# Guards behind operations that read the same data, decayed keys in a buffer of their own, score halves ahead of the next decay part

## Chip, cores and metric

The kernel runs on 1 core of one Trainium2 chip. The metric is the device time of one launch in microseconds (us); lower is better. Differences of about 1% are what a measurement of this kernel can tell from no change.

## What is computed

Three layers over 4 sequences of 768 tokens, 8 heads of 48: a gated linear attention, a dense SiLU layer and a layer of 8 experts of which each token takes one.

```python
for t in range(S):                       # attention, per batch and head
    state = alpha[t, :, None] * state + outer(k[t], v[t])
    y[t] = q[t] @ state
h = x @ w_in                             # x: y of all heads, 3072 x 384
x2 = (h * sigmoid(h)) @ w_out            # d_ff 2048
e = argmax(norm(x2) @ norm(expert_emb).T / tau)
out = gate * (relu(x2 @ w1[e]) @ w2[e])  # 8 experts, 1024 wide
```

## The kernel before

The engines are PE (matrix), DVE (vector), ACT (scalar), POOL (GpSimd) and SP, which issues DMAs. Numbers are kept as pairs of fp16 parts (high and low), so a product is three matmuls.

**Stages.** The dense layer goes over 8 blocks of 384 tokens (`block(j)`), each with 16 steps f: `mm1` makes 128 columns of h (9 matmuls), ACT forms the SiLU and its high part, DVE the low part (line 1084), `mm2` multiplies by w_out (9 matmuls). Attention goes over 24 chunks n of 128 tokens of one sequence; three chunks make one block of x. Chunks 0 to 2 run alone at the start; the others are put between the dense steps: `att_steps` is a generator, and `pump` advances it at up to two points of each f, so the attention of later blocks runs while PE multiplies for the present one. Weights of w_in and w_out are converted in block 0 (`Conv`), those of the experts from block 2 on (`weight1`, `weight2`: a DMA into a staging tile, then `split_after`: ACT makes the high part, DVE the low part). After block 7 follow the expert tiles.

**One chunk** (from chunk 6 on, `n >= NF`, parts in fp16). `att_C`: scores of K and Q into two PSUM banks, ACT copies them to S, POOL sets the upper triangle to zero. `att_S`: ACT and DVE split S into `ss`. `att_A` of the *next* chunk: transpose of alpha (PE), the running product P (DVE scan), its inverse R (DVE), two ACT reductions of P and R into `junk` for a range check (`att_G`), the end factors `pe` (POOL). `att_Bk`, `att_Bq`: transposes of k and q, K = k·R and Q = q·P on DVE. `att_KT`: POOL multiplies K in place by the end factor, ACT and POOL split it into `kd`, and a DMA transposes `kd` into KT. `att_D`: output yp = qs·st + ss·vs. `att_U`: the state update up = KT·vs. Seven steps (yields) per chunk: C; A of n+1 with S and KT of n; Bk; D first half; D second half; move, V and Bq; U.

**What sets the order.** Each engine runs its instructions in one fixed row. The rows are made when the program is built, by a scheduler that goes by the order of the program and its own estimates of when data will be there; `behind(ins, before)` forces an order within an engine. A reduction into a `guard` table (is the data in the range the fp16 parts can hold?) is an ordinary instruction in such a row. For every third chunk `att_V` puts three reductions of the freshly loaded q, k, v tiles (`guard_nat`, line 801); `weight1` puts one for each of the 8 experts' first staging tiles (`guard_w`, line 682). PSUM tiles of the attention come from one pool of three banks in turn (`bank`): a new tile waits until the one three before it has been read.

## Time and profile before

| | |
|---|---|
| time before, median of 3 runs | 791.33 us (789.27 to 795.85) |
| the profiled execution | 792.25 us, of which the span of the profile is 790.6 us |
| PE matmul busy | 748.7 us (95%), 5554 records |
| DVE / ACT / POOL busy | 496.2 / 413.0 / 223.5 us |
| mean granted TensorE clock | 0.991 of full speed |

The span runs from the first to the last instruction. A busy PE is not PE at its peak: ends of matmuls are modelled. "Idle before, releaser" names what ended a wait. Lines are those of the kernel before.

### The profile page before, as it was taken

The page shows a single profiled execution, that of the slowest core. Times are in us where ns is not written, and L with a number is a line of the kernel's source. Part 1 is how long each engine was busy: PE and PEld are TensorE (multiplying, and loading weights), DVE is VectorE, ACT ScalarE, POOL GpSimd, SP SyncE. Part 2 cuts the span into 40 slices and gives each one's busy share as a digit, 9 for nine tenths or more (in the row PEclk, how much of TensorE's full clock was granted, in tenths as well). Part 3 has the DMA queues.
Part 4 walks back from the last instruction along what each step waited for, and adds up shares of the span by engine and source line. Part 5 has one row for each costly group of instructions (what it writes and reads, how often), then busy time and mean ns, then how long its engine had stood idle before and what let it go on. Part 6 is the DMA issues. An engine that isn't in the chain of part 4 may idle for free. (4 is left out here: it accounts for less than half of the span.)

```text
span 790.6 us, 16507 instructions
## 1 busy us (share of the span) xinstructions
PE 748.7 (95%) x5554; PEld 469.7 (59%) x5554; DVE 496.2 (63%) x1446; ACT 413.0 (52%) x931; POOL 223.5 (28%) x322
## 2 busy tenths in 40 slices
PE   7888999999989899999999999999899999999995
PEld 5756777676656566656756655555345555555553
DVE  6599966787677977987877597485761212121211
ACT  3455655666655756766766695577532222222221
POOL 3301113554443553445243112041142111111101
PEclk9999999999999999999999999999999999999998
DMA  9699222444356545645432356157667665676562
GB/s 192 143 287 300 50 55 57 94 89 83 88 117 108 108 109 115 136 101 112 102 96 72 92 172 202 41 161 204 163 162 171 127 112 120 112 119 114 118 104 45
DMA packets 241100, 97.94 MB, mean 124 GB/s; under 512 B 222041, under 2 KB 230398, under 8 KB 240880
## 3 DMA queue, kind: packets, MB, share of 16 engines
q1 hardware_dynamic: 237424, 85.58, 50.2%
q0 software_dynamic: 3584, 11.18, 4.2%
q8 instruction: 51, 0.84, 0.4%
q14 instruction: 41, 0.34, 0.1%
HBM read 58.39 MB, written 12.16 MB: 89 GB/s over the span
## 5 line engine op out<-in xcount | busy, mean ns | idle before, releaser
L1098 PE MATMUL o<-wo_h,w2l 128*128 128x392 f16 x528 | 146.7, 331 | 2.1 <-DVE w2l L1084 1.8
L1426 DVE SCALAR_TENSOR_TENSOR work<-hp,work 128x512 f16<-128x512 f32 x56 | 38.7, 692 | 143.3 <-ACT work L1425 143.3
L1075 PE MATMUL hp<-w2l,wi_h 128*128 128x384 f16 x480 | 120.3, 326 | 0.0
L1098 PEld LDWEIGHTS <-w2l 128*128 128x128 f16 x792 | 75.9, 98 | 51.4 <-DVE w2l L1084 3.0
L1419 PE MATMUL hp<-w1h,xT 128*128 (+1 forms) x384 | 100.0, 379 | 4.6 <-DVE work L1426 3.1
L1075 PEld LDWEIGHTS <-wi_h 128*128 128x128 f16 x768 | 73.8, 98 | 48.4 <-issue 2.0
L1098 PE MATMUL o<-wo_l,w2l 128*128 128x392 f16 x264 | 87.5, 331 | 0.0
L1419 PEld LDWEIGHTS <-xT 128*128 128x128 f16 (+1 forms) x576 | 50.2, 101 | 61.7 <-issue 7.1
L1075 PE MATMUL hp<-w2l,wi_l 128*128 128x384 f16 x240 | 78.2, 326 | 0.0
L1458 POOL DMA_INDIRECT out_dram<-ob,mt x28 | 27.8, 993 | 168.4 <-ACT ob L1455 158.8
L1075 PE MATMUL hp<-w2h,wi_h 128*128 128x384 f16 x288 | 70.6, 326 | 2.4 <-DMA w2h<-ys 1.2
L1425 ACT ACTIVATE work<-hp 128x512 f16<-128x512 f32 x56 | 33.4, 597 | 73.1 <-PE hp L1419 62.9
L1084 DVE SCALAR_TENSOR_TENSOR w2l<-w2l 128x384 f16<-128x384 f32 x88 | 51.8, 591 | 24.5 <-ACT w2l L1083 24.2
L1098 PE MATMUL o<-wo_h,g 128*128 128x392 f16 x240 | 65.8, 329 | 0.3 <-DVE g L1084 0.2
L1419 PE MATMUL hp<-w1l,xT 128*128 (+1 forms) x192 | 63.7, 379 | 0.0
L1455 ACT ACTIVATE ob<-po,s 128x384 f32<-128x384 f32 x28 | 16.3, 581 | 86.1 <-PE po L1447 78.6
L1082 ACT ACTIVATE w2l<-hp 128x384 f32<-128x384 f32 x88 | 42.6, 484 | 31.8 <-PE hp L1075 28.4
L1075 PEld LDWEIGHTS <-wi_l 128*128 128x128 f16 x384 | 37.5, 98 | 24.6 <-DVE wi_l L585 1.9
L1098 PEld LDWEIGHTS <-g 128*128 128x128 f16 x360 | 34.6, 98 | 23.4 <-DVE g L1084 1.1
L1083 ACT ACTIVATE w2l<-w2l 128x384 f16<-128x384 f32 x88 | 45.6, 522 | 4.5 <-PE o L1098 3.0
L841 POOL TENSOR_SCALAR_AFFINE_SELECT S<-S 128x512 f32<-128x512 f32 x48 | 32.7, 705 | 52.8 <-ACT S L840 52.6
L1447 PEld LDWEIGHTS <-work 128*128 128x128 f16 (+1 forms) x384 | 33.5, 101 | 23.6 <-DMA work<-work 1.5
(309 smaller groups left out, 1578.1 us busy)
## 6 DMA issues: line engine op xcount, KB each, us to landing
work<-in_moe_w_dram SPq DMA_DIRECT2D x24, 512.0 KB
work<-in_moe_w_dram SPq DMA_DIRECT2D x30, 384.0 KB
w1h<-in_moe_w_in_dram SPq DMA_DIRECT2D x6, 768.0 KB
nat_a<-in_alpha_dram SPq DMA_DIRECT2D x23, 192.0 KB
nat_k<-in_k_dram SPq DMA_DIRECT2D x23, 192.0 KB
nat_q<-in_q_dram SPq DMA_DIRECT2D x23, 192.0 KB
nat_v<-in_v_dram SPq DMA_DIRECT2D x23, 192.0 KB
w1h<-in_moe_w_out_dram SPq DMA_DIRECT2D x5, 768.0 KB
```

The costliest lines, as they stand in the source:

```text
L841: nc.gpsimd.affine_select(out=s, in_=s, pattern=[[0, NPAIR], [1, 128]], compare_op=ALU.is_ge, fill=0.0, base=0, channel_multiplier=-1,)
L1075: ins = nc.tensor.matmul(out=hp, lhsT=wi[a][f // 2][:, c, (f % 2) * 128:(f % 2 + 1) * 128], rhs=x[:, c, :], start=(n == 0), stop=(n == 3 * ...
L1082: nc.scalar.activation(out=g, in_=hp, func=ACTF.Silu, scale=1.0 / (SX * SWI))
L1083: lead["a"] = nc.scalar.activation(out=gh, in_=g, func=ACTF.Copy, scale=SG)
L1084: lead["g"] = nc.vector.scalar_tensor_tensor(out=gl, in0=g, scalar=SG, in1=gh, op0=ALU.mult, op1=ALU.subtract)
L1098: nc.tensor.matmul(out=acc[t], lhsT=a[:, ts], rhs=wo[w][f // 2][:, f % 2, :], start=(f == 0 and n == 0), stop=(f == KF - 1 and n == 2),)
L1419: nc.tensor.matmul(out=hp[ts], lhsT=xT[:, a, ts], rhs=w1s[w][c][:, e if isinstance(e, int) else bass.ds(e, 1), fs], start=(n == 0), stop=( ...
L1425: lead["a"] = nc.scalar.activation(out=hs[:, 0], in_=hp, func=ACTF.Relu)
L1426: lead["g"] = nc.vector.scalar_tensor_tensor(out=hs[:, 1], in0=hp, scalar=0.0, in1=hs[:, 0], op0=ALU.max, op1=ALU.subtract)
L1447: nc.tensor.matmul(out=po[ts], lhsT=hT[c // 4][:, at + ts.start:at + ts.stop], rhs=w2s[w][c][:, e if isinstance(e, int) else bass.ds(e, 1) ...
L1455: nc.scalar.activation(out=ob, in_=po, func=ACTF.Copy, scale=d["fac"], accum_out=guard("finite", 0.0, ALU.not_equal))
L1458: lead["o"] = nc.gpsimd.indirect_dma_start(out=out[:, :], out_offset=bass.IndirectOffsetOnAxis(ap=d["row"], axis=0), in_=ob, in_offset=Non ...
```

## The change

No operation is added or removed: on every engine the same instructions stand in another order, and the DMAs are the same.

1. *Guards.* The reductions of q, k, v are now ordered `behind` the operation that reads the same tile (`seen`), and those of the experts' weights behind the low part of their split. The two reductions of P and R (`att_G`) are issued after Bq instead of inside A, and behind the latest SiLU high part.
2. *Decayed keys.* `att_KT` for fp16 chunks becomes `att_Kd` (the product, into a buffer `Kd` of its own, right after Bk) and `att_kd` (the split and the DMA transpose, in the step of D's first half), both for chunk n+1 during chunk n; K goes from two buffers to one.
3. *Score halves.* `att_S(n)` stands ahead of `att_A(n + 1)`, and `att_Bq` is a step of its own ahead of D, with the split of Q and of the state (`att_Bs`) left where Bq was. A chunk has eight steps.

```diff
--- before.py
+++ after.py
@@ -622,7 +622,7 @@
                         )
                 hi, lo = wo["h"][self.i][:, :, DM:NA], wo["l"][self.i][:, :, DM:NA]
                 nc.scalar.activation(out=hi, in_=self.pl, func=ACTF.Copy)
-                nc.vector.tensor_sub(out=lo, in0=self.pl, in1=hi)
+                lead["s"] = nc.vector.tensor_sub(out=lo, in0=self.pl, in1=hi)
 
         def conv_w(i):
             c = Conv(i)
@@ -653,6 +653,7 @@
             )
             behind(a, lead["a"])
             behind(d, lead["g"])
+            return d
 
         held, newest = [], [0]
 
@@ -677,11 +678,11 @@
 
                 def convert():
                     held.pop(0)
-                    split_after(st, SW1, w1s["h"][c][:, e, :], w1s["l"][c][:, e, :])
+                    low = split_after(st, SW1, w1s["h"][c][:, e, :], w1s["l"][c][:, e, :])
                     if c == 0:
-                        nc.vector.tensor_reduce(
+                        behind(nc.vector.tensor_reduce(
                             out=guard("w1", 2.0 ** -6), in_=st[:, 0:64], axis=AXX, op=ALU.max, apply_absolute_value=True
-                        )
+                        ), low)
                 return convert
             return begin, c
 
@@ -699,12 +700,12 @@
                     if pooled:
                         split_pool(st, SW2, hi, lo, lead["a"])
                     else:
-                        split_after(st, SW2, hi, lo)
+                        low = split_after(st, SW2, hi, lo)
                     if c == 0:
-                        nc.vector.tensor_reduce(
+                        behind(nc.vector.tensor_reduce(
                             out=guard("w2", 2.0 ** -8), in_=st[:, :, 0:64], axis=mybir.AxisListType.XY, op=ALU.max,
                             apply_absolute_value=True,
-                        )
+                        ), low)
                 return convert
             return begin, c
 
@@ -764,7 +765,9 @@
             P, R = d["P"], d["R"]
             for t in (P, R):
                 junk = a2.tile([128, NPAIR, 128], mybir.dt.bfloat16, tag="junk", name="junk", bufs=1)
-                nc.scalar.activation(out=junk, in_=t, func=ACTF.Copy, accum_out=guard("decay", PMAX, ALU.is_gt))
+                ins = nc.scalar.activation(out=junk, in_=t, func=ACTF.Copy, accum_out=guard("decay", PMAX, ALU.is_gt))
+                if "a" in lead:
+                    behind(ins, lead["a"])
 
         def att_pe(n):
             d = ch[n]
@@ -777,15 +780,24 @@
         def att_A(n):
             att_A1(n)
             att_A2(n)
-            att_G(n)
             att_pe(n)
+
+        def seen(n, nm, ins):
+
+            if n % TPB == 0 and not strict[0]:
+                red = nc.vector.tensor_reduce(
+                    out=guard("nat", 2.0 ** -14), in_=ch[n][nm][:, 0, 0:D], axis=AXX, op=ALU.max,
+                    apply_absolute_value=True,
+                )
+                behind(red, ins)
 
         def att_Bk(n, k=0):
             d = ch[n]
             pk = transpose4(flat(d["k"]), k)
-            K = a2.tile([128, NPAIR, 128], FP32, tag="K", name="K")
-            nc.vector.tensor_mul(out=K, in0=pk, in1=d["R"])
+            K = a2.tile([128, NPAIR, 128], FP32, tag="K", name="K", bufs=1)
+            ins = nc.vector.tensor_mul(out=K, in0=pk, in1=d["R"])
             d["K"] = K
+            seen(n, "k", ins)
 
         def att_V(n):
             d = ch[n]
@@ -793,22 +805,20 @@
                 vs = d["vs"] = a2.tile([128, 2, H * D], FP16, tag="vs", name="vs")
                 src = flat(d["v"])
                 nc.scalar.activation(out=vs[:, 0], in_=src, func=ACTF.Copy, scale=SV)
-                nc.vector.scalar_tensor_tensor(
+                seen(n, "v", nc.vector.scalar_tensor_tensor(
                     out=vs[:, 1], in0=src, scalar=SV, in1=vs[:, 0], op0=ALU.mult, op1=ALU.subtract
-                )
-            if n % TPB == 0:
-                for nm in "qkv":
-                    nc.vector.tensor_reduce(
-                        out=guard("nat", 2.0 ** -14), in_=d[nm][:, 0, 0:D], axis=AXX, op=ALU.max,
-                        apply_absolute_value=True,
-                    )
-
+                ))
         def att_Bq(n, k=0):
             d = ch[n]
             pq = transpose4(flat(d["q"]), k)
             Q = a2.tile([128, NPAIR, 128], FP32, tag="Q", name="Q", bufs=1)
-            nc.vector.scalar_tensor_tensor(out=Q, in0=d["P"], scalar=PCLIP, in1=pq, op0=ALU.min, op1=ALU.mult)
+            ins = nc.vector.scalar_tensor_tensor(out=Q, in0=d["P"], scalar=PCLIP, in1=pq, op0=ALU.min, op1=ALU.mult)
             d["Q"] = Q
+            seen(n, "q", ins)
+
+        def att_Bs(n):
+            d = ch[n]
+            Q = d["Q"]
             if n >= max(B, NF):
                 qs = d["qs"] = a2.tile([128, 2, NPAIR, 128], FP16, tag="qs", name="qs", bufs=1)
                 nc.scalar.activation(out=qs[:, 0], in_=Q, func=ACTF.Copy)
@@ -855,22 +865,25 @@
 
         def att_KT(n):
             d = ch[n]
-            if n // B == CPB - 1:
-                return
-            K = d["K"]
-            if n < NF:
-                pk = transpose4(K.rearrange("p a t -> p (a t)"))
-                KT = d["KT"] = a2.tile([128, NPAIR, 128], FP32, tag="KT", name="KT32")
-                nc.scalar.activation(out=KT, in_=pk, func=ACTF.Copy)
-                return
+            pk = transpose4(d["K"].rearrange("p a t -> p (a t)"))
+            KT = d["KT"] = a2.tile([128, NPAIR, 128], FP32, tag="KT", name="KT32")
+            nc.scalar.activation(out=KT, in_=pk, func=ACTF.Copy)
+
+        def att_Kd(n):
+
+            d = ch[n]
+            Kd = d["Kd"] = a2.tile([128, NPAIR, 128], FP32, tag="Kd", name="Kd", bufs=1)
             wide = d["pe"][:, 0].rearrange("r (p o) -> r p o", o=1).to_broadcast([128, NPAIR, 128])
-            nc.gpsimd.tensor_tensor(out=K, in0=K, in1=wide, op=ALU.mult)
+            nc.gpsimd.tensor_tensor(out=Kd, in0=d["K"], in1=wide, op=ALU.mult)
+
+        def att_kd(n):
+            d = ch[n]
+            Kd = d.pop("Kd")
             kd = a2.tile([128, 2, NPAIR, 128], FP16, tag="kd", name="kd", bufs=1)
-            nc.scalar.activation(out=kd[:, 0], in_=K, func=ACTF.Copy)
-            nc.gpsimd.tensor_sub(out=kd[:, 1], in0=K, in1=kd[:, 0])
-            KT = a2.tile([128, 2 * NPAIR, 128], FP16, tag="KT", name="KT")
+            behind(nc.scalar.activation(out=kd[:, 0], in_=Kd, func=ACTF.Copy), lead["a"])
+            nc.gpsimd.tensor_sub(out=kd[:, 1], in0=Kd, in1=kd[:, 0])
+            KT = d["KT"] = a2.tile([128, 2 * NPAIR, 128], FP16, tag="KT", name="KT")
             nc.sync.dma_start_transpose(out=KT, in_=kd.rearrange("p s a t -> p (s a t)"))
-            d["KT"] = KT
 
         THREE = ((0, 0), (0, 1), (1, 0))
 
@@ -913,7 +926,9 @@
                         )
             if g == 1:
                 ys = d["ys"] = a2.tile([128, 2, H * D], FP16, tag="ys", name="ys")
-                lead[n - 1] = split(yp, SX / (SQ * SST), ys[:, 0], ys[:, 1])
+                ins = split(yp, SX / (SQ * SST), ys[:, 0], ys[:, 1])
+                if n < NF:
+                    seen(n, "v", ins)
 
         def att_move(n):
             b, t = divmod(n, TPB)
@@ -1021,7 +1036,8 @@
             c0.logits()
             att_load(3, "qv")
             strict[0] = False
-            att_V(0)
+            for nm in "kqv":
+                seen(0, nm, lead["s"])
             att_load(4, "akqv")
 
         def att_steps():
@@ -1031,33 +1047,44 @@
             att_Bk(3)
             att_load(5, "k")
             yield
+            att_G(3)
             att_V(3)
             att_Bq(3)
+            att_Bs(3)
             att_load(5, "q")
             yield
             for n in range(3, NCH):
                 more = n + 1 < NCH
+                decayed = NF <= n + 1 < NCH - B
                 att_C(n)
                 yield
+                att_S(n)
                 if more:
                     att_A(n + 1)
                     att_load(n + 3, "a")
-                att_S(n)
-                att_KT(n)
+                if n < NF:
+                    att_KT(n)
                 yield
                 if more:
                     att_Bk(n + 1)
                     att_load(n + 3, "k")
+                    if decayed:
+                        att_Kd(n + 1)
                     yield
+                    att_Bq(n + 1)
+                    att_load(n + 3, "q")
+                    yield
+                    att_G(n + 1)
                 att_D(n, 0)
+                if decayed:
+                    att_kd(n + 1)
                 yield
                 att_D(n, 1)
                 yield
                 att_move(n)
                 if more:
                     att_V(n + 1)
-                    att_Bq(n + 1)
-                    att_load(n + 3, "q")
+                    att_Bs(n + 1)
                     yield
                 att_U(n)
                 if 0 < n < NF:
```

The first place is ACT's row in a chunk that runs during block 1 (S, ss: scores and their parts; kd: parts of decayed keys; junk: the range reductions; hp to g and w2l: the SiLU of a dense step). Before:

```order
L840 ACTIVATE S<-sc_1796 128x512
L840 ACTIVATE S<-sc_1797 128x512
L869 ACTIVATE kd<-K 128x512
L767 ACTIVATE junk,guard_decay<-P 128x512
L853 ACTIVATE ss<-S 128x512 x2
L1082 ACTIVATE g_179<-hp 128x384
L1083 ACTIVATE g_179<-g_179 128x384
L767 ACTIVATE junk,guard_decay<-R 128x512
L814 ACTIVATE qs<-Q 128x512
L817 ACTIVATE st<-state_198 128x384
```

Now:

```order
L850 ACTIVATE S<-sc_1813 128x512
L850 ACTIVATE S<-sc_1814 128x512
L863 ACTIVATE ss<-S 128x512
L768 ACTIVATE junk,guard_decay<-P 128x512
L863 ACTIVATE ss<-S 128x512
L1109 ACTIVATE g_179<-hp 128x384
L1110 ACTIVATE g_179<-g_179 128x384
L768 ACTIVATE junk,guard_decay<-R 128x512
L1109 ACTIVATE w2l_178<-hp 128x384
L1110 ACTIVATE w2l_178<-w2l_178 128x384
L883 ACTIVATE kd<-Kd 128x512
```

The high part of the keys (line 869, now 883) has left the place between the scores and their parts. On POOL, one chunk of the same stage before (AFFINE_SELECT is the triangle, pend the end factors):

```order
L867 TENSOR_TENSOR K<-K,pend 128x512
L841 AFFINE_SELECT S<-S 128x512 x2
L773 TENSOR_SCALAR pend<-P 128x4 x2
L870 TENSOR_TENSOR kd<-K,kd 128x512
L953 TENSOR_TENSOR state_198<-state_198,pend 128x384
L815 TENSOR_TENSOR qs<-Q,qs 128x512
```

Now:

```order
L851 AFFINE_SELECT S<-S 128x512 x2
L776 TENSOR_SCALAR pend<-P 128x4 x2
L968 TENSOR_TENSOR state_198<-state_198,pend 128x384
L877 TENSOR_TENSOR Kd<-K,pend 128x512
L884 TENSOR_TENSOR kd<-Kd,kd 128x512
L825 TENSOR_TENSOR qs<-Q,qs 128x512
```

The triangle is no longer behind the product of the keys; product and low part of the keys stand behind the state's product.

The second place is DVE's row where a chunk begins (P and R: decay; w2l, g: low parts of the dense step). Before:

```order
L796 SCALAR_TENSOR_TENSOR vs<-nat_v_195,vs 128x384
L1084 SCALAR_TENSOR_TENSOR w2l_178<-w2l_178 128x384 x2
L801 TENSOR_REDUCE guard_nat<-nat_v_195 128x1
L749 SCALAR_TENSOR_TENSOR P<-ptr,pmin 128x128 x4
L758 RECIPROCAL R<-P 128x128
L760 TENSOR_TENSOR R<-ptr,R 128x128 x2
```

Now:

```order
L539 SCALAR_TENSOR_TENSOR ys,guard_finite<-yp,ys 128x384
L808 SCALAR_TENSOR_TENSOR vs<-nat_v_196,vs 128x384
L788 TENSOR_REDUCE guard_nat<-nat_v_196 128x1
L1111 SCALAR_TENSOR_TENSOR w2l_178<-w2l_178 128x384
L1111 SCALAR_TENSOR_TENSOR g_179<-g_179 128x384
L750 SCALAR_TENSOR_TENSOR P<-ptr,pmin 128x128 x4
L759 RECIPROCAL R<-P 128x128
```

The reduction of a v tile no longer stands ahead of a scan of P; it stands behind the low part `vs` that reads the same tile.

The third place is PE's row in the first half of D of that chunk. Before:

```order
L910 MATMUL yp<-vs,ss 128x48
L741 MATMUL ptr<-ident,nat_q_181 128x128 x4
L1075 LDWEIGHTS wi_h_167
L1075 MATMUL hp<-w2l_177,wi_h_167 128x384
L910 LDWEIGHTS ss
L910 MATMUL yp<-vs,ss 128x48
L903 LDWEIGHTS qs
L903 MATMUL yp<-st,qs 128x96
```

Now:

```order
L1102 LDWEIGHTS wi_l_173
L1102 MATMUL hp<-w2l_177,wi_l_173 128x384
L916 LDWEIGHTS qs
L916 MATMUL yp<-st,qs 128x96
L916 LDWEIGHTS qs
L916 MATMUL yp<-st,qs 128x96
L916 LDWEIGHTS qs
L916 MATMUL yp<-st,qs 128x96
L923 LDWEIGHTS ss
L923 MATMUL yp<-vs,ss 128x48
```

The transpose of q stood inside D and has moved ahead of it, and the matmuls of D, spread between dense matmuls before, stand together.

## Rows read from the trace of the kernel before

**Rows 1.** Windows: length; busy us (count) PE, PEld, DVE, ACT, POOL; clock; DMA; GB/s.

```profile
60.00:80.00 20.00, 17.14 (x127) 12.06 (x125) 20.00 (x37) 11.57 (x23) 3.91 (x4) 1.00 0.97 289
...
180.00:380.00 200.00, 189.33 (x1650) 124.92 (x1649) 160.61 (x474) 129.77 (x289) 89.75 (x123) 0.99 0.49 106
```

**Rows 2.** Waits of PE from 180 to 380 us: total, times, longest.

```profile
PE yp L910 <- DVE ss L854: 2.6, 5, 1.1
PE up L944 <- DMA KT<-kd: 2.2, 4, 1.3
PE pr L1141 <- DVE state L958: 1.9, 2, 1.1
PE yp L910 <- ACT ss L853: 1.9, 1, 1.9
PE up L944 <- DVE K L787: 0.5, 2, 0.3
PE o L1098 <- DVE w2l L1084: 0.2, 1, 0.2
```

**Rows 3.** Groups of instructions from 180 to 380 us: busy, mean ns, idle before.

```profile
L910 PE MATMUL yp<-vs,ss 128*128 128x48 f16 x242 | 15.6, 187 | 5.0 <-DVE ss L854 2.6 <-ACT ss L853 1.9
...
L944 PE MATMUL up<-vs,KT 128*128 128x96 f16 x120 | 6.8, 206 | 2.8 <-DMA KT<-kd 2.2 <-DVE K L787 0.5
```

**Rows 4.** Waits of DVE from 180 to 380 us.

```profile
DVE guard_w L682 <- DMA work<-in_moe_w_dram: 8.8, 6, 4.2
DVE guard_nat L801 <- DMA nat_v<-in_v_dram: 7.2, 3, 2.6
DVE guard_nat L801 <- DMA nat_k<-in_k_dram: 4.5, 3, 2.2
DVE guard_nat L801 <- DMA nat_q<-in_q_dram: 3.2, 3, 1.3
```

**Rows 5.** Timeline of one chunk: start us, us, instruction, idle before.

```profile
182.53 1.16 PE L830 MATMUL sc<-Q,K 64*128 64x128 f32 x16
...
184.28 0.33 PE L1098 MATMUL o<-wo_l,w2l 128*128 128x392 f16 x1
...
184.44 0.49 PE L1098 MATMUL o<-wo_h,w2l 128*128 128x392 f16 x2
...
185.20 0.63 ACT L869 ACTIVATE kd<-K 128x512 f16<-128x512 f32 x1 [0.39 <-POOL K L867]
...
186.41 0.20 DVE L801 TENSOR_REDUCE guard_nat<-nat_v 128x1 f32<-128x48 f32 x1 [2.14 <-DMA nat_v<-in_v_dram]
...
187.92 0.63 ACT L767 ACTIVATE junk<-P 128x512 bf16<-128x512 f32 x1 [2.08 <-DVE P L749]
...
189.67 0.67 DVE L854 TENSOR_TENSOR ss<-S,ss 128x512 f16<-128x512 f32 x1
189.70 1.33 POOL L953 TENSOR_TENSOR state<-state,pend 128x384 f32<-128x384 f32 x1
189.77 1.23 SPq L872 DMA_TRANSPOSE KT<-kd  x1
...
190.27 0.38 DVE L760 TENSOR_TENSOR R<-ptr,R 128x128 f32<-128x128 f32 x1
190.40 0.25 PE L910 MATMUL yp<-vs,ss 128*128 128x48 f16 x3 [0.41 <-DVE ss L854]
...
190.57 1.01 DVE L854 TENSOR_TENSOR ss<-S,ss 128x512 f16<-128x512 f32 x1
...
193.03 0.68 PE L944 MATMUL up<-vs,KT 128*128 128x96 f16 x12 [0.36 <-DMA KT<-kd]
```

**Rows 6.** Timeline of the chunk with the longest waits.

```profile
232.91 0.22 DVE L682 TENSOR_REDUCE guard_w<-work 128x1 f32<-128x64 f32 x1 [4.22 <-DMA work<-in_moe_w_dram]
...
235.85 0.22 PE L910 MATMUL yp<-vs,ss 128*128 128x48 f16 x2 [1.93 <-ACT ss L853]
```

**Rows 7.** Windows, columns as in Rows 1: the stretch with the lowest clock.

```profile
220.00:240.00 20.00, 17.65 (x169) 12.04 (x167) 14.88 (x35) 12.44 (x26) 6.78 (x9) 0.92 0.64 129
```

## The prediction, made before the changed kernel ran

> **What bounds the kernel now.** I read the page first: PE is busy 95% of the span, so only what stops PE counts. The windows by stage come next. Between 60 and 80 us DVE is busy all 20 us while PE has 2.9 us idle: there the conversion of the dense weights is the bound. Between 180 and 380 us PE is idle 200 - 189.3 = 10.7 us, and no other engine is full: DVE has 160.6 us, ACT 129.8, POOL 89.8 [rows 1]. In this stretch lie the attention chunks with fp16 parts, which is where the change works; the reader should look for who lets PE wait there. The list of PE's waits answers: the output matmuls wait for the score parts (2.6 us by DVE, 1.9 by ACT), the update matmuls for the transposed keys (2.2 by the DMA, 0.5 by K), and the routing matmuls for DVE (1.9) [rows 2].
>
> Why are parts and keys late? One chunk of the timeline shows it. DVE stands 2.14 us before a range reduction of a v tile that has not landed. Behind it stands the scan of P, so ACT waits 2.08 us before the reduction of P into junk, and behind that stand the score parts: DVE ends the second of them at 190.57 + 1.01 = 191.58 us, 7.9 us after the scores ended (182.53 + 1.16 = 183.69). PE waits 0.41 us for them, and 0.36 us for the keys, whose DMA could only be issued at 189.77 [rows 5]. The worst chunk has the same shape with a wait of 4.22 us before a reduction of an expert's weights; PE then waits 1.93 us [rows 6], and it is in that stretch that the clock falls to 0.92 [rows 7]. In all DVE stands 8.8 + 7.2 + 4.5 + 3.2 = 23.7 us before such reductions in the stretch [rows 4]. They are 0.2 us of work each; the wait is the cost.
>
> **The change part by part.** Each engine's row holds the same instructions before and now, so no busy time is added or saved; only waits can go or come.
>
> *Guards.* A reduction behind the operation that has just read the same tile cannot wait for that tile's load. The 23.7 us of waits on DVE lose their cause. Cost of the move itself: nothing, as the 0.2 us of each reduction was paid already. Part of the wait for an expert's weights may come back as a wait of the split, which needs the same transfer; bounds 0 and 8.8 us of DVE time. I take it near 0 for PE, since the split stands behind the dense step's low part and ends no chunk.
>
> *Decayed keys.* Before, ACT's row had the keys' high part between the scores and their parts: 0.63 us, after a wait of 0.39 us for POOL [rows 5]. Both leave the path of the score parts. Their new cover: the keys of chunk n+1 are split while PE runs D of chunk n and are wanted after D of n+1. The 120 update matmuls are 10 chunks in 200 us [rows 3], so the transposing DMA gets a chunk, on average some 20 us, where it had 193.03 - 189.77 = 3.3 us [rows 5]. On SP's queue it now stands behind the next k and q loads instead of ahead of them; with that much slack I cost this at 0. If the cover were gone it would cost the 2.2 us of the row again.
>
> *Score halves and the place of Q.* In PE's row, from the last score matmul to the first use of a score part, there were 24 to 31 dense matmuls in the 14 chunks with keys; now there are 37 to 46. A lone dense matmul takes 0.33 us in the records and two take 0.49, so each further one is 0.16 us [rows 5]. The cover grows from some 28 x 0.16 = 4.5 us to 41 x 0.16 = 6.6 us, besides the transposes. The parts were ready after 7.9 us in a chunk with a late load; without the 2.14, the 0.39 and the 0.63 that is 4.7 us. The waits for the parts should end.
>
> *What is late next.* PSUM tiles go round three banks. With Q's transpose ahead of D, the output tile now takes the bank of the transposed alpha, which the last step of R reads, where it took one that ACT frees early. R ended at 190.27 + 0.38 = 190.65, 7.0 us after the scores, or 4.8 us without the late load [rows 5]; one more score part of 0.67 us ahead of it makes 5.5 us. The fewest matmuls ahead of D, 37 x 0.16 = 5.9 us, still cover that, by 0.4 us. Below nothing this cannot be, as a later R stops PE directly. I allow three chunks a new wait of 0.5 us, the size of the waits in rows 5 (0.41, 0.36): 1.5 us.
>
> *A place where the modelled end matters.* The idle column gives 5.0 us ahead of the output matmuls and 2.8 us ahead of the update matmuls, 7.8 us [rows 3]. A lone matmul is recorded for 0.33 us where its successor could start after 0.16 or 0.17, so each stall hides some 0.16 us under a busy PE; with 5 + 1 + 4 + 2 = 12 stalls [rows 2] that is 1.9 us more. The Trainium skill (Perfetto Trace Analysis, Tensor Engine Instruction) says that the end of a matmul in the profile is estimated from its size, not observed; by that the idle column is a lower bound, and the sum without the 1.9 us would end at 784.3 us. The trace agrees as far as 0.33 and 0.49 go.
>
> *Clock.* 0.92 over 20 us is 1.6 us of lost pace [rows 7]. It follows the stall of 1.93 us [rows 6], the longest of the stretch [rows 2], so I count it as that one's; bounds 0 and 1.6, and I take 1.6 because no other stretch of that kind has it.
>
> *The rest.* Routing's 1.9 us stay. In block 0 the same DVE work is only in another order; bounds -2 to +2 us of the 2.9 us idle there [rows 1], taken as 0. The expert tiles keep their rows.
>
> Sum: 7.8 + 1.9 + 1.6 - 1.5 = 9.8 us less. The profiled execution took 792.25 us (span 790.6), so 782.4 us, which is 8.9 us (1.1%) under the median of 791.33. A measurement of this kernel can tell about 1%, 7.9 us, from no change; the bound of "faster" lies at 783.4 us, close to the forecast.
>
> **Rivals.**
>
> *Half of it comes back at the bank of alpha.* DVE's score part took 1.01 us where its twin took 0.67, while POOL's state product ran [rows 5]. If such a 0.34 us hits R in all 14 chunks with keys and eats the slack, PE loses 14 x 0.34 = 4.8 us more: 787.2 us. For it: a slack of 0.4 us. Against it: the products of the keys have moved away from the scores on POOL.
>
> *The waits only move.* The late loads stay late, and ACT's and DVE's splits of the experts' weights wait for them in the same rows. If the 8.8 of the 23.7 us [rows 4] return to PE in proportion, 0.37 x 11.3 = 4.2 us: 786.6 us. For it: the split's transfer is the guard's. Against it: the splits stood in the rows before as well, and were waited for then.
>
> *More than the sum.* Routing's waits go too (1.9 us [rows 2]) and block 0 gains its 2 us: 778.5 us.
>
> *Slower: the keys hold the dense step.* POOL's product and low part of the keys now run when DVE makes the dense step's low parts (line 1084) for `mm2`. A POOL operation of this kind runs 1.33 us, and the two DVE records beside and without it differ by 0.34 us [rows 5]. Two operations that each held a dense low part for their whole 1.33 us on PE's path would cost 14 x 2.66 = 37 us, less the cover between `mm1` and `mm2`, 9 matmuls of the next step or more (9 x 0.16 = 1.4 us for each): 14 x (2.66 - 1.4) = 17.6 us, so 792.25 - 9.8 + 17.6 = 800.0 us. It decides from 1.4 us a chunk, where 9.8 us are lost and 7.9 more. Against it: the longest wait of a dense matmul for that line in the stretch is 0.2 us [rows 2], with as many POOL operations running. The Trainium skill (SBUF — State Buffer, Who interferes with whom) says that a DVE instruction with two SBUF inputs and a GpSimd instruction that reads SBUF exclude each other for a whole instruction; the trace agrees in direction (1.01 against 0.67 us).
>
> **How the numbers follow.** The forecast's case, most stalls of the stretch gone, 0.60 (780 to 785.5 us); half back at the bank 0.13; waits only move 0.08; more than the sum 0.13; slower 0.06. The likeliest gives 782.4 us. The range leaves out the slower case and the far ends of the others: 777.5 to 789. Faster by over 1%: the 0.13 of the larger gain and 0.4 of the forecast's 0.60, as its upper part lies above 783.4: 0.53. Slower 0.06; the same 0.41.
>
> **What would show it.** In the profile of the changed kernel DVE should have no wait before a guard reduction on a load; PE's waits at the output and update matmuls in this stretch should fall from 7.2 us listed to under 2; PE's idle time there from 10.7 us to some 3; and the clock should be 1.00 throughout. A new line "output tile waits for R" would speak for the first rival, dense matmuls waiting for line 1084's operation for the last. The forecast is wrong if the waits go and the span does not follow, which would mean that the stages after it take the time back, or if PE now waits in block 0.

## The result and the profile after

The changed kernel takes 788.68 us (median of 20 runs, 782.61 to 797.90) against 793.38 us of the kernel before, run beside it (20 runs, 789.02 to 797.12). Three of the 20 runs of the changed kernel lie over 1.5% above its fastest and are left out of the ratio, as is done for all kernels here; the other 17 have a median of 786.49 us. The ratio is 0.9914, 95% interval 0.9894 to 0.9935: 0.9% faster, which is within the 1% that the prediction called no change. The two medians are 6.3 and 4.1 us above the 782.4 us forecast. The profiled execution has a span of 788.1 us, 2.5 us less than before.

The lines of the code have moved: the dense step's matmuls L1075 and L1098 are now L1102 and L1125, its low part L1084 is L1111, the output L910 is L923, the update L944 is L959, the score parts L853 and L854 are L863 and L864, the reductions L801 are L788, the scan of P L749 is L750, the last step of R L760 is L761, the experts' matmuls L1419 and L1447 are L1446 and L1474.

In the stretch on which the prediction rests, the waits went as forecast. The windows, in the columns of [rows 1]:

```profile
180.00:380.00 200.00, 198.09 (x1825) 134.41 (x1824) 168.58 (x493) 138.53 (x310) 96.92 (x129) 1.00 0.56 116
220.00:240.00 20.00, 20.00 (x180) 13.67 (x177) 15.90 (x37) 13.38 (x28) 10.79 (x15) 1.00 0.57 139
```

PE's idle time between 180 and 380 us went from 10.7 to 1.9 us, and 1825 matmuls fit where 1650 did. The list of PE's waits there (total, times, longest) no longer names the output or the update:

```profile
PE o L1125 <- DVE lg L1155: 0.7, 1, 0.7
PE hp L1102 <- ACT w2l L1109: 0.3, 1, 0.3
PE o L1125 <- DVE w2l L1111: 0.3, 1, 0.3
PE pr L1168 <- DVE state L973: 0.3, 1, 0.3
PE o L1125 <- DVE g L1111: 0.3, 1, 0.3
```

The two groups of [rows 3] have no idle time before them now:

```profile
L923 PE MATMUL yp<-vs,ss 128*128 128x48 f16 x288 | 14.1, 183 | 0.0
L959 PE MATMUL up<-vs,KT 128*128 128x96 f16 x144 | 8.4, 205 | 0.0
```

And DVE waits for no load ahead of a reduction, where it stood 23.7 us [rows 4]. What is left in its list is work of the other engines; the one guard in it waits for an activation:

```profile
DVE P L750 <- PE ptr L742: 7.6, 7, 1.6
DVE g L1111 <- ACT g L1110: 6.9, 5, 2.2
...
DVE guard_g L1115 <- ACT w2l L1109: 0.9, 1, 0.9
```

One chunk of the timeline, beside [rows 5]:

```profile
194.87 1.16 PE L840 MATMUL sc<-Q,K 64*128 64x128 f32 x16
...
198.11 0.63 ACT L768 ACTIVATE junk<-P 128x512 bf16<-128x512 f32 x1
...
198.76 0.83 POOL L968 TENSOR_TENSOR state<-state,pend 128x384 f32<-128x384 f32 x1
198.98 1.16 DVE L864 TENSOR_TENSOR ss<-S,ss 128x512 f16<-128x512 f32 x1
...
200.78 0.68 DVE L864 TENSOR_TENSOR ss<-S,ss 128x512 f16<-128x512 f32 x1
...
201.38 0.38 DVE L761 TENSOR_TENSOR R<-ptr,R 128x128 f32<-128x128 f32 x1
...
203.84 0.31 PE L923 MATMUL yp<-vs,ss 128*128 128x48 f16 x6
```

The second score part is ready at 200.78 + 0.68 = 201.46, 5.4 us after the scores' end (196.03), where it was 7.9; the first matmul that reads a part stands at 203.84, 7.8 us after it. The slack is over 2 us in this chunk. R ends at 201.38 + 0.38 = 201.76, 5.7 us after the scores, also ahead of the output.

**Where the gain went.** A table of milestones shows it. The end of block 0 is the start of the first silu of block 1 (line 1082, now 1109: at 133.24 and at 140.99 us), the end of block 5 that of block 6; behind that come the last two dense blocks and the experts. In us, of the profiled executions (rounded one by one):

| | block 0 ends at | blocks 1 to 5 | the rest | span |
|---|---|---|---|---|
| before | 133.2 | 325.7 | 331.6 | 790.6 |
| after | 141.0 | 310.6 | 336.6 | 788.1 |

So the stages with the fp16 chunks gave 15.1 us, more than the forecast's sum, and 7.8 us of it were given back in block 0, 4.9 behind the chunks. In block 0 two things differ. One is a wait of PE that was not there. In PE's and DVE's rows of the changed kernel (`pt` is a transposed half of a dense weight, `ptr` a transposed chunk):

```profile
126.47 0.60 PE L742 MATMUL ptr<-ident,K 128*128 128x128 f32 x4
126.84 1.10 DVE L1111 SCALAR_TENSOR_TENSOR w2l<-w2l 128x384 f16<-128x384 f32 x1
126.90 0.49 PE L610 MATMUL pt<-ident,w1l 128*128 128x128 f32 x3
127.86 1.20 DVE L761 TENSOR_TENSOR R<-ptr,R 128x128 f32<-128x128 f32 x3
129.12 0.55 PE L610 MATMUL pt<-ident,w1l 128*128 128x128 f32 x3 [1.73 <-DVE R L761]
```

Alpha's transpose, the keys' and the weight's first half hold the three banks; the second half wants alpha's bank again, and that is free only when R has ended. The other is the clock. The 20 us windows from 60 us on:

```profile
60.00:80.00 20.00, 18.11 (x109) 11.98 (x108) 19.53 (x36) 9.33 (x18) 2.75 (x4) 0.83 1.02 292
80.00:100.00 20.00, 19.38 (x116) 14.15 (x114) 16.09 (x31) 10.14 (x22) 0.83 (x1) 0.83 0.19 53
100.00:120.00 20.00, 20.00 (x153) 15.70 (x152) 13.03 (x27) 10.33 (x23) 1.73 (x4) 1.00 0.21 41
120.00:140.00 20.00, 17.34 (x142) 14.13 (x141) 11.56 (x41) 9.85 (x28) 8.74 (x14) 1.00 0.43 83
```

A clock of 0.83 over 20 us is 3.4 us of lost pace (20 x 0.17), at the lower of the two levels (1.2 GHz) for some 7 us; twice here. Whether that is the change or chance, and which part of the change brings the wait, the profile alone can't say.

### The profile page after: what moved, and what is told of

Read it like the earlier page. It is cut to its first block, busy times and chain, and to the rows that moved or that the text cites. A ratio compares the mean times of both kernels' runs of the same rounds, so it can differ in the third digit from the quotient of the medians.

```text
span 788.1 us, 16535 instructions
## 1 busy us (share of the span) xinstructions
PE 751.4 (95%) x5554; PEld 475.5 (60%) x5554; DVE 493.1 (63%) x1446; ACT 412.5 (52%) x931; POOL 222.0 (28%) x322
## 5 line engine op out<-in xcount | busy, mean ns | idle before, releaser
L1125 PE MATMUL o<-wo_h,w2l 128*128 128x392 f16 x528 | 146.3, 331 | 3.5 <-DVE w2l L1111 2.7
L1102 PE MATMUL hp<-w2l,wi_h 128*128 128x384 f16 x480 | 119.0, 326 | 1.2 <-DMA w2l<-ys 0.9
L1125 PEld LDWEIGHTS <-w2l 128*128 128x128 f16 x792 | 75.7, 98 | 54.2 <-DVE w2l L1111 4.2
L1102 PEld LDWEIGHTS <-wi_h 128*128 128x128 f16 x768 | 75.1, 99 | 53.2 <-issue 4.1
L1446 PE MATMUL hp<-w1h,xT 128*128 (+1 forms) x384 | 101.4, 383 | 3.2 <-DVE work L1453 2.9
L1446 PEld LDWEIGHTS <-xT 128*128 128x128 f16 (+1 forms) x576 | 50.6, 102 | 60.8 <-issue 6.8
L1125 PE MATMUL o<-wo_l,w2l 128*128 128x392 f16 x264 | 87.0, 330 | 0.0
L1102 PE MATMUL hp<-w2l,wi_l 128*128 128x384 f16 x240 | 78.2, 326 | 0.0
L1102 PE MATMUL hp<-w2h,wi_h 128*128 128x384 f16 x288 | 73.1, 337 | 2.3 <-ACT wi_h L581 1.2
L1111 DVE SCALAR_TENSOR_TENSOR w2l<-w2l 128x384 f16<-128x384 f32 x88 | 53.0, 602 | 23.2 <-ACT w2l L1110 22.8
L1125 PE MATMUL o<-wo_h,g 128*128 128x392 f16 x240 | 66.3, 329 | 0.3 <-DVE g L1111 0.3
L1446 PE MATMUL hp<-w1l,xT 128*128 (+1 forms) x192 | 64.3, 382 | 0.0
L851 POOL TENSOR_SCALAR_AFFINE_SELECT S<-S 128x512 f32<-128x512 f32 x48 | 31.1, 671 | 82.3 <-ACT S L850 82.0
L1102 PEld LDWEIGHTS <-wi_l 128*128 128x128 f16 x384 | 38.1, 99 | 24.9 <-issue 1.0
L1474 PEld LDWEIGHTS <-work 128*128 128x128 f16 (+1 forms) x384 | 33.5, 101 | 26.9 <-DMA work<-work 5.3
L1125 PEld LDWEIGHTS <-g 128*128 128x128 f16 x360 | 34.7, 98 | 22.9 <-DVE g L1111 0.9
```

Of the source, the lines that this page charges most:

```text
L851: nc.gpsimd.affine_select(out=s, in_=s, pattern=[[0, NPAIR], [1, 128]], compare_op=ALU.is_ge, fill=0.0, base=0, channel_multiplier=-1,)
L1102: ins = nc.tensor.matmul(out=hp, lhsT=wi[a][f // 2][:, c, (f % 2) * 128:(f % 2 + 1) * 128], rhs=x[:, c, :], start=(n == 0), stop=(n == 3 * ...
L1111: lead["g"] = nc.vector.scalar_tensor_tensor(out=gl, in0=g, scalar=SG, in1=gh, op0=ALU.mult, op1=ALU.subtract)
L1125: nc.tensor.matmul(out=acc[t], lhsT=a[:, ts], rhs=wo[w][f // 2][:, f % 2, :], start=(f == 0 and n == 0), stop=(f == KF - 1 and n == 2),)
L1446: nc.tensor.matmul(out=hp[ts], lhsT=xT[:, a, ts], rhs=w1s[w][c][:, e if isinstance(e, int) else bass.ds(e, 1), fs], start=(n == 0), stop=( ...
L1474: nc.tensor.matmul(out=po[ts], lhsT=hT[c // 4][:, at + ts.start:at + ts.stop], rhs=w2s[w][c][:, e if isinstance(e, int) else bass.ds(e, 1) ...
```

## The experiments

The theory was that the new order of the steps costs block 0 what it gives later. Rivals: the clock falls by chance; the guards do it. The numbers of all kernels stand in one table behind the last of them.

**The changed kernel again, unaltered.**

> The changed kernel once more, unaltered: what of its profile is its order, and what is chance? Between 180 and 380 us both theories expect PE busy 198 us of 200 again. Theory A (the new order of the steps in block 0 costs the gain back there): between 40 and 100 us the granted clock falls again to between 0.85 and 0.92, with a wait of over 2 us near 47 us, and the time is 788.7 us within 2, ratio to the kernel before 0.991. Rival B (the clock in block 0 falls by chance): 40 to 100 us at 0.98 or more in this profile, with the same waits in the rows or shorter ones.

786.98 us, ratio 0.9901 (0.9866 to 0.9936). 180 to 380 us is the same again (PE busy 198.0). Block 0 ends at 137.7 us, with the same wait for R (1.6 us, now at 125 us); the wait at 47 us is 0.8 us instead of 2.5. The clock from 40 to 100 us is 0.915, in the range that theory A gave, but from 60 us on the stretches at the lower level lie elsewhere (82 to 89 and 130 to 133 us, none near 70). So the wait for R is there in both executions, and where the clock falls differs between them; how often it falls stayed open.

**Block 0 with the step order of before**, twice.

```
 for n in range(3, NCH):
     ...
     att_C(n)
     yield
+    if n + 1 < NF:    # A, G, KT; Bk; D 0; D 1; move, V, Bq: 7 steps
+        ...
+    else:             # as changed
```

> The changed kernel with the step order of before for chunks 3 to 5, those that run in block 0 (7 steps a chunk, query ahead of nothing, range sums of P and R right after R); everything else as changed. Theory A: block 0 gets its pace of before (40 to 100 us at clock 0.98 or more, PE busy there as before) and 180 to 380 us stays at 198 busy: some 5 us less than the changed kernel, 783.5 us, ratio to before 0.987. Rival B (clock by chance): no change against the changed kernel, 788.7 us, ratio 0.991, the clock low in block 0 in either profile as it falls. Rival C (the guards, or the moved splits, cost block 0): as B, with the clock low here again.

780.49 us, ratio 0.9829 (0.9786 to 0.9872). Block 0 ends at 133.2 us, there is no wait for R, and the clock holds from 60 us on:

```profile
60.00:80.00 20.00, 17.68 (x129) 12.19 (x127) 20.00 (x39) 10.80 (x22) 3.06 (x4) 1.00 1.01 296
80.00:100.00 20.00, 19.99 (x152) 14.74 (x150) 20.00 (x37) 12.23 (x28) 4.03 (x5) 1.00 0.31 72
100.00:120.00 20.00, 20.00 (x160) 16.10 (x159) 14.16 (x34) 11.09 (x25) 3.34 (x6) 1.00 0.25 50
120.00:140.00 20.00, 18.32 (x132) 12.99 (x131) 12.01 (x67) 11.38 (x31) 8.60 (x13) 1.00 0.35 71
```

> The kernel of the run with the old step order in block 0, unaltered, once more: is its gain over the changed kernel (780.5 against 787 to 788.7 us) its order, or chance? If the order: 780.5 us within 1.5, ratio to before 0.983, and at most one stretch at the lower clock level (1.2 GHz) between 40 and 140 us (one of 3 us in its first profile; two or three of 3 to 7 us in those of the changed kernel). If chance: 784 to 788 us, ratio 0.989 to 0.991, and two or three such stretches.

782.50 us, 2 us above the first run where at most 1.5 was expected, ratio 0.9864 (0.9823 to 0.9905); from 45 to 140 us one stretch at the lower level, 3.4 us at 125 us; block 0 ends at 132.4 us. The gain in block 0 is the order's, or that of something that came with it: the old order has 7 steps a chunk, the new one 8.

**Guards alone**, on the kernel before.

```
-    nc.vector.tensor_reduce(out=guard("w1", ...), in_=st[:, 0:64], ...)
+    behind(nc.vector.tensor_reduce(out=guard("w1", ...), in_=st[:, 0:64], ...), low)
...
+    seen(n, "k", ins)     # and "q", "v": behind the operation that reads the tile
...
-    att_G(n)              # in att_A
+    att_G(n + 1)          # ahead of att_D(n, 0)
```

> The kernel before with the guards part alone: reductions behind the operation that reads the same data, the range sums of P and R behind the dense step's activation. Step order, keys and score halves as before. By the prediction's steps: DVE has no wait before a guard on a load between 180 and 380 us (23.7 us before); the 2.1 to 4.2 us that late loads cost a chunk go, the keys' high part still stands ahead of the score halves on ACT. So the longest waits at the output (4.5 us listed) mostly go, those at the update by the key transfer (2.2) stay: PE idle there from 10.7 to 4 to 6 us, time 4 to 6 us under before, ratio 0.993 to 0.995. Rival: the guards alone give everything (idle 2 to 3 us, ratio 0.988), the rest of the change nothing. Other rival: they give nothing, because the loads come late for the splits too (idle 9 to 11, ratio 1.00).

787.65 us, ratio 0.9887 (0.9847 to 0.9927): more than expected, and no less than the whole change gives (0.9914). The idle time between 180 and 380 us is 3.9 us, at the lower end of what was expected, and the waits left are the keys' and two for the score parts:

```profile
PE up L952 <- DMA KT<-kd: 1.4, 1, 1.4
PE yp L916 <- DVE ss L860: 1.3, 2, 0.7
PE up L952 <- DVE K L798: 0.9, 1, 0.9
```

Blocks 1 to 5 take 313.4 us, 12.3 of the 15.1 us that the whole change gives there. Of the parts tried alone this is the largest.

**Order and keys without the guards.** The changed kernel with those edits undone.

> The changed kernel with the guards put back where they stood before; keys in their own buffer, query ahead and score halves first as changed. By the prediction's steps: DVE waits for late loads again (some 24 us between 180 and 380 us), but 37 matmuls or more instead of 24 cover the chain, so PE idle there is 4 to 6 us against 10.7 before and 1.9 changed; time 790 to 791 us, if block 0 loses as in the changed kernel, ratio 0.996. Rival: the longer cover alone takes all waits (idle 2 to 3 us), ratio 0.991 as the whole change. Theory A also expects block 0 with a clock under 0.92 here, as the order does that and not the guards; rival C expects it at 0.98 or more.

794.05 us, ratio 0.9995 (0.9964 to 1.0025): nothing in the whole time. Late loads hold DVE again (8.7 and 8.0 us in the two longest lines), and 37 matmuls or more of cover don't hide it: PE is idle 8.7 us between 180 and 380 us, not the 4 to 6 expected.

```profile
DVE guard_nat L802 <- DMA nat_v<-in_v_dram: 8.7, 4, 4.1
DVE guard_w L683 <- DMA work<-in_moe_w_dram: 8.0, 6, 2.1
...
PE yp L911 <- DVE R L761: 2.1, 3, 1.4
PE o L1115 <- DVE lg L1145: 1.8, 1, 1.8
```

The first line of PE is the wait of the output for alpha's bank that the prediction feared. It is there when loads are late, three times, 2.1 us; with the guards moved it is not. Block 0 ends at 136.8 us, with the wait for R (1.6 us): that loss does not need the guards. The clock from 60 to 140 us is 0.96, between what theory A and rival C said. Blocks 1 to 5 take 318.3 us, 7.4 less than before: order and keys do give something there without the guards, and it is lost in block 0 (3.6) and behind block 5 (2.6). The gains of the parts don't add up either: 12.3 and 7.4 us alone, 15.1 together.

**The query's place, in block 0 alone.**

```
-    att_Bq(n + 1)
-    att_load(n + 3, "q")
+    if n + 1 >= NF:       # chunks 4, 5: behind att_D, as before
+        att_Bq(n + 1)
+        att_load(n + 3, "q")
     yield                 # 8 steps stay
```

> The changed kernel with one thing moved: for chunks 4 and 5, in block 0, the query's transpose and product stand behind the output again, as before; the 8 steps a chunk, the place of the range sums and of the keys stay. Theory Q (in block 0 the query ahead of the output makes transposes wait for the bank that the transposed alpha holds until R ends, a wait of 1.6 to 1.9 us near 125 us, and the clock falls behind such waits): 780.5 us as with the whole old order, ratio 0.983, no wait of PE for R over 0.5 us in block 0. Rival P (the pace: 8 steps a chunk instead of 7 push the chunks' work to the end of the block): as the changed kernel, 787 to 788.7 us, ratio 0.990.

788.19 us, ratio 0.9916 (0.9884 to 0.9948): the theory that the query's place costs block 0 fell. The wait for R is there without it, longer, and the clock goes down with it:

```profile
120.42 0.60 PE L742 MATMUL ptr<-ident,K 128*128 128x128 f32 x4
120.85 0.49 PE L610 MATMUL pt<-ident,w1l 128*128 128x128 f32 x3
...
123.17 0.78 DVE L761 TENSOR_TENSOR R<-ptr,R 128x128 f32<-128x128 f32 x2
124.00 0.83 PE L610 MATMUL pt<-ident,w1l 128*128 128x128 f32 x3 [2.66 <-DVE R L761]
...
120.00:140.00 20.00, 17.14 (x84) 14.68 (x82) 7.58 (x21) 6.32 (x18) 6.74 (x11) 0.66 0.37 72
```

(The last line is from the windows: a clock of 0.66, so 6.8 us of lost pace in 20.)

**The query behind the output everywhere, 7 steps.** Guards, keys and score halves as changed.

> The changed kernel without the query ahead of the output anywhere: guards moved, keys decayed in their own buffer, score halves ahead of the next decay part, and 7 steps a chunk; the query's transpose and product behind the output as before. By the prediction's steps the query's place is what lengthens PE's cover from 24 to 37 matmuls. If that cover is needed: waits for the score halves come back between 180 and 380 us, PE idle there 4 to 5 us (guards alone left 3.8, the changed kernel 2.0). If it is not: PE idle there 2 to 2.5 us as in the changed kernel. In block 0 theory Q expects no wait of over 0.5 us for R, and then 780.5 to 783.5 us, ratio 0.983 to 0.987; if the block 0 loss is anything else, 787 us, ratio 0.990.

781.52 us, ratio 0.9849 (0.9814 to 0.9884). No wait for R in block 0, which ends at 130.4 us. Blocks 1 to 5 take 314.0 us, as with the guards alone (313.4), and PE is idle 3.7 us between 180 and 380 us, between the two cases expected. The keys' own buffer and the score halves add no time to the guards that this shows. They did remove the waits that they were made for (2.3 us for the keys and 1.3 for the score parts with the guards alone, now none and 0.2), but others stand in their place, the two longest at the routing (1.1 us) and at a dense output (1.0). Against the 310 us of the changed kernel, what is missing is the query ahead of the output and the eighth step; that the query's gain is its cover for the score parts is not shown, as they are hardly waited for without it.

**The kernel before again.**

> The kernel before, unaltered, for a second profile of it: how much of the difference between two profiles is chance? Both theories expect 793.4 us within 4, PE idle between 180 and 380 us from 9 to 12 us again, waits of DVE before guards on loads over 15 us in that stretch. Open is what the clock does: if stretches at the lower level fall by chance, their places differ from the first profile (118 and 236 us); if they belong to places, they are there again.

791.46 us in its one run. The waits of [rows 2] and [rows 4] are there again (PE 2.5 and 1.5 us at the output, 2.7 and 0.5 at the update; DVE 22.3 us ahead of guards on loads), but the clock is 1.00 where [rows 7] have 0.92:

```profile
180.00:380.00 200.00, 188.95 (x1670) 123.98 (x1669) 160.34 (x473) 129.10 (x288) 89.19 (x122) 1.00 0.50 107
```

Blocks 1 to 5 take 325.6 us all the same. From 45 us on, stretches at the lower level lie at 54, 108 and 559 us here, at 118 and 237 us in the first profile: these places differ between two executions of one kernel, so they are chance.

**One yield less for chunks 4 and 5.** The pace of before with the new order.

```
     att_load(n + 3, "q")
-    yield
+    if n + 1 >= NF:
+        yield
```

> The changed kernel with one yield less for chunks 3 and 4 in block 0: 7 steps each instead of 8, as before, the query still ahead of the output. Theory P (the pace: with 8 steps the alpha and K transposes of a chunk fall into the same dense step as the two transposed halves of a dense weight, which then wait for alpha's bank until R ends, 1.6 to 2.7 us near 125 us, and the clock falls around it): that wait goes under 0.5 us, block 0 ends (129th silu order: first silu of block 1) at 131 to 134 us instead of 138 to 143, time 780 to 782.5 us, ratio 0.985. Theory Q (place of the query): 787 to 789 us, ratio 0.991; it has already failed once (query behind, 8 steps: 788.2).

783.15 us, ratio 0.9862 (0.9827 to 0.9896). The wait for R shrinks to 0.3 us. Block 0 ends at 134.9 us, a little later than expected, after 7 us at the lower level from 107 us on; the time is 0.7 us above what was expected as well.

**One yield more in the old order.**

```
     att_move(n)
+    yield
     att_V(n + 1)
```

> The old step order in block 0 (780.5 and 782.5 us in two runs) with one yield more for chunks 3 and 4, so 8 steps each. Theory P: the loss of the changed kernel comes back without its order: a wait of 1.5 us or more of transposes for R between 115 and 130 us, block 0 ends at 137 us or later, time 786 to 789 us, ratio 0.990. Rival (order and pace only together, or the lot of one schedule): 780 to 783 us, ratio 0.985.

784.02 us, ratio 0.9887 (0.9864 to 0.9910), between what theory and rival said. The profile, which is of the slowest of the six runs (788.62 us), shows what theory P expected of it: block 0 ends at 140.9 us, and the wait for R is back, as PE's list from 60 to 140 us has it:

```profile
PE pt L610 <- DVE R L761: 1.9, 1, 1.9
```

**7 steps for every chunk**, the query ahead of the output everywhere.

```
     att_load(n + 3, "q")
-    yield
     att_G(n + 1)
```

> The changed kernel with 7 steps for every chunk: the yield behind the query's product is gone, the order of operations stays. Theory P for block 0: as with 7 steps there alone. After block 0 it shows what the eighth step is worth between 180 and 380 us: if the cover ahead of the output is the place of the query, PE idle there stays near 2 us and the time is 780 to 782 us; if it is the eighth step that spreads the work, waits come back, PE idle 3.5 to 5 us (3.7 with the query behind and 7 steps) and 782 to 785 us.

780.31 us, ratio 0.9861 (0.9830 to 0.9891). No wait for R of PE's transposes, though the output has one of 0.3 us. Between the transposes of alpha and keys (`nat_a`, `K`) and the weight's halves now stand those of the next k and q, in PE's row:

```profile
117.00 0.60 PE L742 MATMUL ptr<-ident,nat_a 128*128 128x128 f32 x4
117.44 0.60 PE L742 MATMUL ptr<-ident,K 128*128 128x128 f32 x4
118.37 0.60 PE L742 MATMUL ptr<-ident,nat_k 128*128 128x128 f32 x4
121.30 0.60 PE L742 MATMUL ptr<-ident,nat_q 128*128 128x128 f32 x4
...
124.92 1.08 PE L610 MATMUL pt<-ident,w1l 128*128 128x128 f32 x6
```

Block 0 ends at 134.5 us, and the later stages keep all they had:

```profile
180.00:380.00 200.00, 198.02 (x1821) 133.92 (x1819) 168.01 (x494) 137.70 (x308) 96.41 (x128) 1.00 0.56 116
```

So the gain behind block 0 does not need the eighth step. Against the query behind the output, with 7 steps too, the query's place makes 4.4 us in blocks 1 to 5 (314.0 to 309.6).

**Query behind and 7 steps in block 0, the rest as changed.**

> A version meant to beat both: chunks 4 and 5 in block 0 with the query behind the output and 7 steps, later chunks as in the changed kernel (query ahead, 8 steps), guards and keys as changed everywhere. From the milestones: block 0 as with the query behind and 7 steps (ends at 130.4 us), the chunks behind it as changed (310.3 us from there to the end of the attention chunks against 314.0 with the query behind), the rest 335 us: 776 to 780 us in the fast runs, ratio 0.980 to 0.983. Rival (each schedule draws its own luck in block 0, and nothing adds up): 781 to 788 us.

783.46 us, ratio 0.9873 (0.9845 to 0.9901): no addition. Its profile has three stretches at the lower level in block 0 (at 67, 108 and 128 us), and blocks 1 to 5 take 312.0 us, as with one yield less (311.9), against 310. In both PE is idle 3.4 us between 180 and 380 us, with the query ahead there and 8 steps as in the changed kernel: the query's place alone does not bring the 310, it also matters at what point of the dense steps the chunks arrive. A miss; parts of milestones of other schedules don't add up to a microsecond.

All profiles side by side. "Wait for R" is that of the weights' transposes in block 0, "clock" the mean granted clock from 60 to 140 us, the stages as above; of the runs with another schedule the ratio to the kernel before. The stages are those of one execution each; for the guards alone, for the old order with 8 steps and for the query behind in block 0 with 8 steps it was the slowest of that kernel's runs.

| kernel | steps in block 0 | wait for R | clock | block 0 ends | blocks 1 to 5 | the rest | ratio |
|---|---|---|---|---|---|---|---|
| before, twice | 7 | none | 0.98, 0.98 | 133.2, 132.6 | 325.7, 325.6 | 331.6, 331.5 | 1 |
| guards alone | 7 | none | 0.94 | 134.5 | 313.4 | 341.5 | 0.9887 |
| old order in block 0, twice | 7 | none | 1.00, 0.98 | 133.2, 132.4 | 310.1, 310.1 | 335.0, 334.3 | 0.9829, 0.9864 |
| query behind | 7 | none | 1.00 | 130.4 | 314.0 | 336.2 | 0.9849 |
| one yield less | 7 | 0.3 | 0.96 | 134.9 | 311.9 | 333.9 | 0.9862 |
| 7 steps everywhere | 7 | none | 0.96 | 134.5 | 309.6 | 333.4 | 0.9861 |
| query behind in block 0, 7 steps | 7 | none | 0.91 | 136.0 | 312.0 | 335.0 | 0.9873 |
| after, twice | 8 | 1.7, 1.6 | 0.91, 0.94 | 141.0, 137.7 | 310.6, 310.2 | 336.6, 337.7 | 0.9914, 0.9901 |
| without the guards | 8 | 1.6 | 0.96 | 136.8 | 318.3 | 334.2 | 0.9995 |
| query behind in block 0, 8 steps | 8 | 2.7 | 0.89 | 142.7 | 309.8 | 337.6 | 0.9916 |
| old order, 8 steps | 8 | 1.9 | 0.89 | 140.9 | 310.3 | 335.8 | 0.9887 |

## Why the prediction was right and where it was not

**Guards: right, and larger than its share.** The waits on loads went, as the step said, and none came back at the splits. Alone they give 12.3 us of the 15.1; the query's place gives 3 to 4 more where the chunks arrive well, though not shown to do so as the longer cover that the prediction counted on; keys and score halves on top of the guards give nothing that shows.

**Idle time at output and update, 7.8 us: right.** It is 0.0 now. The step for the bank of alpha (1.5 us) was not needed: with punctual loads the output has no wait for R in these blocks; in the chunk shown R ended 5.7 us after the scores, where 5.5 was forecast. Rival *half comes back at the bank of alpha* had the right mechanism at the wrong place; the wait stands in block 0, at a dense weight's transpose. Routing's 1.9 us, which were to stay, are 0.3 us.

**The hidden stalls, 1.9 us: too small.** The windows over blocks 1 to 5 hold almost the same matmuls: before, 133 to 459 us, 2775 in 315.3 us of busy time, 10.7 us idle; after, 141 to 452 us, 2773 in 308.8, 2.2 idle. Idle time fell by 8.5 us, but busy time by 6.5 as well, for the same work. The second profile of the kernel before has the clock at 1.00 all through the stretch, and its busy time is 6.1 us above the changed kernel's.

```profile
133.00:459.00 326.00, 315.33 (x2775) 209.37 (x2774) 254.81 (x734) 213.28 (x468) 134.64 (x187) 0.99 0.45 100
...
133.00:459.00 326.00, 314.89 (x2775) 208.10 (x2774) 254.22 (x729) 213.06 (x466) 133.94 (x185) 1.00 0.46 100
...
141.00:452.00 311.00, 308.79 (x2773) 208.13 (x2772) 251.49 (x728) 212.41 (x465) 133.29 (x182) 1.00 0.48 105
```

(The first two lines are of the kernel before, the third of the changed one.) Busy time that goes with no work gone I take for stall hidden under modelled ends. The Trainium skill (Perfetto Trace Analysis, Tensor Engine Instruction) calls the end of a matmul estimated; the trace agrees, with 6.1 us, none of it clock, where the prediction counted 1.9.

**The clock, 1.6 us: not shown.** It was counted as following a stall of 1.93 us. In the second profile of the kernel before the clock holds through this stretch, with waits of up to 2.0 us, and the stages are as long (325.6). That term was one execution's chance.

**Block 0, 0 with bounds of 2 us: the step that failed.** The prediction looked at DVE's work there and found it only reordered. It did not follow the new number of steps. `pump_j` draws up to two steps of the generator in each dense step, so 8 steps a chunk instead of 7 move a chunk's transposes against the weights' conversion, which is drawn by its own pump. At 8 steps the transposes of alpha and keys near the end of block 0 come right ahead of both halves of a weight in the turn of the banks, four tiles on three, and PE's row stands behind R. With 7 steps the transposes of k and q, or that of k and the output, lie between them and the halves. All five profiles with 8 steps have this wait (1.6 to 2.7 us), none of the nine with 7 has it over 0.32; taking the yield out removes it with the order kept, putting one into the old order brings it back. The block ends at 139.8 us in the mean of the five, 133.5 of the nine, two of the five being the slowest runs of their kernels. Of these 6.3 us the wait itself is 1.9; the clock is an estimated 3.8, as its mean from 60 to 140 us is 0.919 against 0.967 (80 x 0.048). That the wait makes the clock fall is not shown: in four of the five it falls within 5 us of it, in one only well ahead of it, and elsewhere in the block the place changes from profile to profile.

In times, the four experiments with the guards moved and 8 steps in block 0 (the changed kernel is two of them) have ratios of 0.9887 to 0.9916, mean 0.9905; the six with the change's other parts and 7 steps 0.9829 to 0.9873, mean 0.9856: 3.9 us at 793. The intervals of single pairs overlap, the ratios of the two groups don't. The timed runs bear out the two shares: each has its span and mean granted clock on record, and (1 - clock) x span is its lost pace. Over the runs that the ratios use, the first group has a mean (of its experiments' means) of 786.8 us with 14.4 of lost pace, the second of 782.1 with 11.2. So 3.2 of 4.7 us go with the clock, and 1.5 are left for the wait and all else.

**The other rivals.** Nothing moved to the splits, and the slower case, POOL's keys holding the dense low parts, did not come: PE has two waits of 0.3 us for that line in the stretch. A reading and a sum behind these rivals are off. The score part of 0.67 us in [rows 5] did not run without POOL's state product but beside it, having begun 0.03 us ahead of it; the one of 1.01 us began while it ran. In the changed kernel it is the same: 1.16 us for the part that begins 0.22 us into POOL's 0.83 (198.76 and 198.98 in the timeline above), and seven of its 36 score parts take that long. R still came in time. And the slower case decides from 17.7 / 14 = 1.3 us a chunk, not 1.4.

**The experts, 0: wrong by 2 to 6 us, cause open.** Behind block 5 every variant takes longer than the kernel before, 333.4 to 337.7 us (341.5 in the guards' profile) against 331.6 and 331.5. Part of it, 1.7 or 3.4 us by estimate, is the clock: nine of these twelve profiles have one or two stretches of 3.4 us (or one of 7) at the lower level between 450 and 560 us, the first profile of before none and its second one. Another part is in the list of PE's waits from 560 us on. After:

```profile
PE po L1474 <- DMA work<-work: 4.2, 3, 2.6
...
PE po L1474 <- DMA g<-work: 1.4, 1, 1.4
PE po L1474 <- DMA hb<-work: 1.0, 1, 1.0
```

That is 6.6 us for transposing DMAs, where the same three lines of before have 1.0, 1.2 and 0.9, and 4.7 in the second profile of the changed kernel. What makes these transfers late, when the last 157 of SP's issues, from the end of the chunks on, stand in the same order, was not tried.

So the forecast of 782.4 us was the sum of a gain that was under-counted by 5.3 us (15.1 against 9.8) and two stages taken as 0 that took back 7.8 and 4.9 (4.5 and 6.1 in the second profile). The medians fell by 4.7 and 7.3 us. That 788.68 us lies inside the stated range, 0.3 us under its upper end, is luck in part: the errors have opposite signs. The likeliest outcome by its chances, faster by over 1% (0.53), did not come; the same (0.41) did.

**A version that beats both.** 7 steps for every chunk, one line less than the changed kernel: 780.31 us, ratio 0.9861 to the kernel before (0.9830 to 0.9891), clear of the changed kernel's interval in the result (0.9894 to 0.9935), though not of that of its second run (0.9866 to 0.9936). The old order in block 0 (780.49 and 782.50) and the query behind the output (781.52) can't be told from it.

## What to carry to other kernels

Where a generator feeds one stream of work into another at a fixed pace, a new yield is a change of its own: count the steps, and see beside what each now falls, above all in a stage with a second generator and a shared turn of buffers. A check that reads loaded data stands behind an operation that waits for that data anyway, or the whole engine waits for the load. And before a gain is claimed or missed, divide both profiles at the same milestones of the work: a difference of 2.5 us in the span was +7.8, -15.1 and +4.9.

## What was not expected of the hardware

The same wait does not always bring the clock down. Near 66 us PE waits for ACT's copy of a weight's transposes in eleven of the profiles, 1.4 to 1.8 us from start to start of two matmuls; the clock falls to the lower level right behind it, for 7 us, in five of them, and holds in the other six, among them the old order in block 0 in both its profiles. The size of the wait does not decide it: at 1.40 us it held, at 1.43 to 1.53 it fell, at 1.71 and 1.73 it held, at 1.77 it fell, at 1.82 it held. Not all places are chance, though: all fourteen profiles have a stretch from 20 to 23 us on, and ten have one that begins between 544 and 560 us, around a wait of 3.0 to 4.0 us at the first experts' matmuls; of the four without it two wait 2.8 and 3.0 us there and two 3.2.

A stretch of 7 us costs 3.4 us by estimate. The lost pace of the timed runs shows what that makes. Among the 17 runs of the changed kernel that the ratio uses, the fastest (782.61 us, clock 0.988) lost 9.4 us and the slowest (793.12 us, clock 0.977) 18.2: 8.8 us of lost pace for 10.5 us of time. Most of the spread of that kernel from run to run goes with the clock.
